# Sparse attention with a feed-forward layer: one register load for the six sampled blocks of a tile

## The chip, the cores and the metric

The kernel runs on one core of one Trainium2 chip. The metric is the device time of that core in microseconds; a result is the median of several runs. A core has engines that run their own instruction streams side by side: PE multiplies matrices, DVE, ACT and POOL do elementwise work, and SP only issues transfers. They wait for one another through semaphores, and each works through its own queue strictly in order.

## The reference

Four batches, eight heads, 768 positions, head width 64. Attention is block sparse in blocks of 32 (24 blocks): a query block sees its own block and its two neighbours, the first and the last block, and three sampled blocks; the first and the last query block see everything. The output goes through a feed-forward layer without residual.

```
scores = scale * np.matmul(q, k.transpose(0, 1, 3, 2))
...
for qb in range(n_blocks):
    for kb in sampled_blocks[qb]:
        mask[qb * block:(qb + 1) * block, kb * block:(kb + 1) * block] = True
scores = np.where(mask, scores, -1000000000.0)
...
attn = attn / (np.sum(attn, axis=-1, keepdims=True) + 1e-09)
return np.matmul(attn, v).astype(np.float32)
...
h = x @ w_in
g = np.maximum(0.01 * h, h)
return (g @ w_out).astype(np.float32)
```

The sampled block numbers are an input of shape 24 x 3, int64, so their values are known only when the kernel runs.

## The kernel before, in words

**Tiles.** Two query blocks (64 queries) make a tile. Each batch has 12 tiles: tile 0 holds the first and the last query block and works on all keys; tiles 1 to 11 work on 12 gathered key blocks each, called slots: four of the window (0 to 3), the first and the last block (4, 5) and six sampled ones, three for each query block (6 to 11). So there are 4 x 11 = 44 gathered tiles. A tile is worked on in four units, one for each pair of heads; four tiles make an item, and an item's feed-forward work is done in chunks while later tiles are in attention.

**A unit's path.** Scores on PE (line 628), scale and mask with the row minimum on DVE (637), exponential on ACT (648), the sums' reciprocal on DVE (657), the high half of the normalised probabilities on ACT (663) and their low half on DVE (668), a transposing transfer issued by SP (671), and the product with V on PE (689). Numbers are kept as a high and a low half-precision part. The feed-forward layer has its matmuls in lines 724 and 751, with work on ACT, DVE and POOL between them (731, 735, 740, 741).

**The K gather** (`gather_k`, lines 558 to 582) fills one of two SBUF buffers: DVE copies the window (564), and POOL copies the six sampled blocks (573), each from a position in the transposed keys that stands in a register. For each slot, POOL first loads the register from the table `offs` (572) and checks its range. The function is a generator that yields after every slot; two slots are taken at each step of the main loop.

**The V gather** (`gather_v`, lines 587 to 605) fills one of two SBUF buffers from a scratch copy of V in HBM. SP issues one transfer for the window (593), at each buffer's first use in a batch two for the first and the last block (598), and then, slot by slot, a register load with its check (601) and the transfer that uses it (603).

**The table.** `build_masks` (199) shifts the block numbers left by five on DVE into `offs` (200), 72 words in the order of the input.

**What sets the order.** The builder is given the work in the order in which the main loop writes it, with priorities by step, and fixes each engine's queue before the run. `in_order` (540) adds an order without a semaphore: all instructions of a new group except the last come after the last instruction of the group before the previous one. A group here is one slot: its load, its check and its copy or transfer. A load can so be at most two slots ahead of its use. SP's queue also carries every other transfer: the loads of q, k, v and the weights (455, 464, 405, 286), the transposes of q and k (517, 494) and of the probabilities (671), the swapped copy of q (519, 520), the store of V's scratch (435) and of the results (775 to 779).

Of the kernel before, what the change touches and what calls it, by code (L numbers as in the profile page):

```python
# [14 lines left out]
I32 = mybir.dt.int32  # L15
AF = mybir.ActivationFunctionType
ALU = mybir.AluOpType
# [3 lines left out]
BLOCK = 32  # L21
# [5 lines left out]
SLOTS = 12  # L27
# [34 lines left out]
def tile_block_sparse_attention_ffn(  # L62
# [19 lines left out]
    nc = tc.nc  # L82
    B, H, S, D = q.shape
    DM, FF = w_in.shape
    NB = S // BLOCK
    NR = sampled.shape[1]
# [5 lines left out]
    NT = NB // 2  # L92
# [7 lines left out]
    cst = ctx.enter_context(tc.tile_pool(name="cst", bufs=1))  # L100
# [12 lines left out]
    def bank(name, tag="h"):  # L113
        return ps_1.tile([P, 512], F32, tag=tag, name=name, bufs={"h": 3, "av": 1}[tag])
# [70 lines left out]
    row = tmps[:1, 6:6 + 2 * NB * NR].bitcast(I32)  # L185
    eq = tmps[:NB, 150:150 + NR * NB].rearrange("p (r b) -> p r b", r=NR)
    sels = [tmps[:NB, 222 + P * a:222 + P * (a + 1)].rearrange("p (a b c) -> p a b c", a=2, b=2) for a in range(2)]
    assert 222 + 2 * P <= DM and 6 + 2 * NB * NR <= 150
    offs = cst.tile([1, NB * NR], I32, name="offs")
    mask = cst.tile([P, NT - 1, SLOTS], F32, name="mask")  # L190

    def load_constants():
# [4 lines left out]
        nc.sync.dma_start(out=sb, in_=sampled.bitcast(I32))  # L197

    def build_masks():
        nc.vector.tensor_scalar(  # L200
            out=offs, in0=row.rearrange("p (a b) -> p a b", b=2)[:, :, 0], scalar1=5, scalar2=None,
            op0=ALU.logical_shift_left)
        sf = cst.tile([NB, NR], F32, name="sf")
        nc.vector.tensor_copy(out=sf, in_=sb.rearrange("p (a b) -> p a b", b=2)[:, :, 0])

        ok = cst.tile([NB, NR], F32, name="ok")
        hit = cst.tile([NB, NB], F32, name="hit")
        for r in range(NR):
            nc.vector.tensor_scalar(out=eq[:, r, :], in0=iota, scalar1=sf[:, r:r + 1], scalar2=None, op0=ALU.is_equal)
            nc.vector.tensor_tensor(out=hit, in0=eq[:, r, :], in1=allow, op=ALU.mult)  # L210
            nc.vector.tensor_reduce(out=ok[:, r:r + 1], in_=hit, op=ALU.add, axis=AX.X)
            nc.vector.tensor_tensor(out=allow, in0=allow, in1=eq[:, r, :], op=ALU.max)
        nc.vector.tensor_scalar(out=ok, in0=ok, scalar1=-1.0, scalar2=1.0, op0=ALU.mult, op1=ALU.add)

        at = cst.tile([NB, NT - 1, 2, NR], F32, name="at")
        nc.gpsimd.affine_select(
            out=at.rearrange("p t a r -> p (t a) r"), in_=ok.unsqueeze(1).to_broadcast([NB, NB - 2, NR]),
            pattern=[[-1, NB - 2], [0, NR]], base=-1, channel_multiplier=1,
            compare_op=ALU.is_equal, fill=0.0)
        pm = bank("mask_ps")[:, :(NT - 1) * 2 * NR].rearrange("p (t a r) -> p t a r", t=NT - 1, a=2)  # L220
        for a in range(2):
            sel = sels[a]
            nc.vector.memset(sel, 0.0)
            nc.vector.memset(sel[:, :, a, :], 1.0)
            nc.tensor.matmul(
                pm[:, :, a, :], sel.rearrange("p a b c -> p (a b c)"), at[:, :, a, :], start=True, stop=True)
        nc.vector.tensor_scalar(
            out=mask[:, :, 6:], in0=pm.rearrange("p t a r -> p t (a r)"), scalar1=-1.0, scalar2=-NEG,
            op0=ALU.add, op1=ALU.mult)
        nc.vector.memset(mask[:, :, :6], 0.0)  # L230
        for hh in range(2):
            a, b = (slice(D * hh + BLOCK * i, D * hh + BLOCK * (i + 1)) for i in range(2))
            nc.vector.memset(mask[a, :, 3:4], NEG)
            nc.vector.memset(mask[b, :, 0:1], NEG)
            nc.vector.memset(mask[a, 0:1, 4:5], NEG)
            nc.vector.memset(mask[b, NT - 2:NT - 1, 5:6], NEG)
# [300 lines left out]
    kgs, vgs = {}, {}  # L537
    last_use = {}

    def in_order(key, begin):  # L540

        new = nc.cur_bb.bb.instructions[begin:]
        last = last_use.setdefault(key, deque())
        if len(last) > 1:
            for i in new[:-1]:
                tc.add_manual_dep(i, last[0], mybir.DependencyInfo(
                    mybir.DependencyClass.NoSync, mybir.DependencyReason.DATA), reason="order")
            last.popleft()
        last.append(new[-1].name)

    def sampled_of(T):

        return [(6 + a * NR + r, (2 * T - 1 + a) * NR + r) for a in range(2) for r in range(NR)]

    kgb = [pa.tile([P, H, KEYS], F16, tag=f"kg{i}", name=f"kg{i}", bufs=1) for i in range(2)]
    ends = {}
# [1 line left out]
    def gather_k(b, T):  # L558

        kt = kts[b]  # L560
        n = (b * (NT - 1) + T - 1) % 2
        kg = kgb[n]
        t0 = (T - 1) * Q2
        nc.vector.tensor_copy(out=kg[:, :, :P], in_=kt[:, :, t0:t0 + P])
        if ends.get(n) != b:
            ends[n] = b
            nc.vector.tensor_copy(
                out=kg[:, :, P:P + Q2].rearrange("p h (n l) -> p h n l", l=BLOCK),
                in_=kt.rearrange("p h (n l) -> p h n l", l=BLOCK)[:, :, 0:NB:NB - 1, :])
        for slot, i in sampled_of(T):  # L570
            begin = len(nc.cur_bb.bb.instructions)
            off = nc.gpsimd.value_load(offs[:1, i:i + 1], min_val=0, max_val=S - BLOCK)
            nc.gpsimd.tensor_copy(  # L573
                out=kg[:, :, slot * BLOCK:(slot + 1) * BLOCK], in_=kt[:, :, bass.ds(off, BLOCK)])
            in_order("k", begin)
            yield
        em = pa.tile([P, KEYS], BF16, tag="em", name=f"em_{b}_{T}", bufs=2)
        nc.gpsimd.tensor_copy(
            out=em.rearrange("p (n l) -> p n l", l=BLOCK),
            in_=mask[:, T - 1, :].unsqueeze(2).to_broadcast([P, SLOTS, BLOCK]))  # L580
        kgs[b, T] = kg, em
        yield
# [4 lines left out]
    def gather_v(b, T):  # L587

        n = (b * (NT - 1) + T - 1) % 2
        vg = vgb[n]  # L590
        t0 = (T - 1) * Q2
        place = lambda slot: (slice(slot % 4 * BLOCK, (slot % 4 + 1) * BLOCK), slot // 4)
        nc.sync.dma_start(out=vg[:, 0, :], in_=scr[b][t0:t0 + P, :])
        if vends.get(n) != b:
            vends[n] = b
            for slot, a in ((4, 0), (5, S - BLOCK)):
                ps, c = place(slot)
                nc.sync.dma_start(out=vg[ps, c, :], in_=scr[b][a:a + BLOCK, :])
        for slot, i in sampled_of(T):
            begin = len(nc.cur_bb.bb.instructions)  # L600
            off = nc.sync.value_load(offs[:1, i:i + 1], min_val=0, max_val=S - BLOCK)  # L601
            ps, c = place(slot)
            nc.sync.dma_start(out=vg[ps, c, :], in_=scr[b][bass.ds(off, BLOCK), :])  # L603
            in_order("v", begin)
        vgs[b, T] = vg.rearrange("p c (h x) -> p c h x", h=H)


# [306 lines left out]
    def start_gather(b, T):  # L914
        for hp in range(NP):
            until(("k", b, hp), lambda: (b, hp) in kready)
        gens["kg", b, T] = gather_k(b, T)
        gathers.append(gens["kg", b, T])
# [4 lines left out]
    def start_gather_v():  # L923
        b, T = vq.popleft()
        until(("v", b), lambda: (b, "ready") in scr)
        assert vfree[0] > 0
        vfree[0] -= 1
        gather_v(b, T)
# [14 lines left out]
    for hp in range(NP):  # L943
        load_v(0, hp)
    build_masks()
    start_k(0, 2)
    start_k(0, 3)
# [49 lines left out]
    for u in units:  # L997
        it, ui = u.item, u.k * NP + u.hp
        b, nb = it.b, it.b + 1
# [7 lines left out]
        if nb < B:  # L1007
            g = it.j * 16 + ui
            t = g - (CFG["k_at"] if b else CFG["k_at0"])
# [4 lines left out]
            t = g - CFG["v_at"]  # L1014
# [135 lines left out]
```

## Time and profile before

| what | value |
|---|---|
| runs of the kernel before | 957.5 us median (956.35, 957.5, 960.08) |
| the profiled execution, span from the first to the last instruction | 959.4 us |
| the profiled execution's own time as shown beside it | its span, 959.4 us; nothing further is listed |
| mean granted TensorE clock in it | 0.934 |
| register loads of lines 601 (SP) and 572 (POOL) | 264 each |
| transfers of line 603 (SP), copies of line 573 (POOL) | 264 each |
| transposes of line 671 (SP) | 208 |

The profile lists, for one execution, the busy time of each engine, the chain of work that ended last (followed back from the last instruction to whatever released it), the costliest groups of instructions, who waited for whom, and the transfers. PE is the matmul part of TensorE and PEld its weight loads, which overlap. Instructions that move registers, branch, signal or issue transfers are not counted as busy, so SP's and POOL's queues of such instructions (SPq, POOLq) are seen only in the chain, in the rows of one line and in the timeline. Idle time of an engine that is not the bottleneck costs nothing. L601 is line 601 of the kernel.

### The profile page before, as it was taken

The numbers are of one execution on the slowest core, as the hardware profiler recorded it, in microseconds if no ns is written. First come the engines' busy times: TensorE is split into PE (matmuls) and PEld (weight loads), VectorE is DVE, ScalarE is ACT, GpSimd is POOL, SyncE is SP. The second block draws the span as 40 slices with busy tenths as digits, with TensorE's granted clock in tenths as the row PEclk, the third lists the DMA queues.
The fourth block names the chain that finished last, engine by engine and source line by source line (L and its number), as shares of the span: only waits on it lengthen the run. The fifth ranks groups of instructions, "written<-read, shape, count | busy, mean of one in ns | idle before, by whom it ended". The sixth has DMA issues, their size and how long they took to land.

```text
span 959.4 us, 21885 instructions
## 1 busy us (share of the span) xinstructions
PE 775.6 (81%) x7020; PEld 485.8 (51%) x7020; DVE 609.4 (64%) x1643; ACT 493.8 (51%) x1061; POOL 328.3 (34%) x469
## 2 busy tenths in 40 slices
PE   1325445878988989997988979897989999999998
PEld 1213233535556555554655545555555655655675
DVE  4986778897576957455766556556666566655221
ACT  4564774755564646445545545555555554545121
POOL 0133544562213424423422344332423334432221
PEclk9996555999998999998999999998998999999999
DMA  9995986957767676685676868766785755556200
GB/s 212 279 269 117 271 169 141 204 113 151 152 167 147 125 147 148 147 146 122 134 175 133 161 121 144 164 135 132 162 164 104 151 135 131 119 114 124 34 23 23
DMA packets 336625, 139.39 MB, mean 145 GB/s; under 512 B 299389, under 2 KB 311678, under 8 KB 336510
## 3 DMA queue, kind: packets, MB, share of 16 engines
q1 hardware_dynamic: 336510, 137.99, 67.8%
q8 instruction: 55, 0.90, 0.4%
q14 instruction: 60, 0.49, 0.2%
HBM read 65.57 MB, written 12.58 MB: 81 GB/s over the span
## 4 chain that ended last, share of the span: by engine, by line
PE 41%; DMA 19%; DVE 16%; SPq 9%; issue 7%; ACT 7%; POOL 0%; ACTq 0%; DVEq 0%
PE h L724 17%; PE o L751 15%; DMA pt<-pp 9%; PE s L628 4%; PE av L689 4%; DVE pp L668 3%; DMA kt<-k_k 3%; DVE p L637 3%; SPq L601 2%; ACT p L648 2%; DMA qs_q<-qa_q 2%; ACT pp L663 2%; SPq L603 2%; SPq L671 2%; DMA W<-in_moe_w_in_dram 1%
## 5 line engine op out<-in xcount | busy, mean ns | idle before, releaser
L724 PE MATMUL h<-x,W 128*128 128x256 f16 x2304 | 288.0, 280 | 1.7 <-DVE k_tot L136 1.2
L751 PE MATMUL o<-W,g 128*128 128x512 f16 x1152 | 280.0, 384 | 4.8 <-DVE g L740 2.7
L724 PEld LDWEIGHTS <-W 128*128 128x128 f16 x2304 | 225.1, 101 | 52.9 <-issue 11.0
L668 DVE SCALAR_TENSOR_TENSOR pp<-p,r,pp 128x384 f16<-128x384 f32 x208 | 151.6, 737 | 128.2 <-ACT pp L663 127.5
L741 POOL TENSOR_TENSOR g<-ht,g 128x512 f16<-128x512 f32 x96 | 115.1, 1199 | 263.6 <-DVE g L740 170.7
L663 ACT ACTIVATE pp<-p,r 128x384 f16<-128x384 f32 x208 | 122.0, 608 | 143.2 <-DMA pt<-pp 111.9
L648 ACT ACTIVATE p<-p,mx 128x384 f32<-128x384 f32 x208 | 126.4, 608 | 98.2 <-DVE mx L637 61.6
L573 POOL COPY kg<-kt 128x256 f16 x264 | 128.5, 508 | 133.9 <-PE s L628 73.2
L751 PEld LDWEIGHTS <-g 128*128 128x128 f16 x1152 | 103.3, 98 | 135.0 <-issue 22.8
L689 PE MATMUL av<-pt,vg 128*64 128x128 f16 x2112 | 100.7, 231 | 47.6 <-DMA pt<-pp 44.8
L637 DVE CUSTOM_DVE_ANT_0 p<-s,em,nsc 128x384 f32<-128x384 f32 x176 | 106.1, 609 | 33.2 <-PE s L628 32.5
L689 PEld LDWEIGHTS <-vg 128*64 128x64 f16 x2112 | 79.5, 115 | 88.8 <-issue 76.4
L735 DVE SCALAR_TENSOR_TENSOR ht<-h,gd,ht 128x512 f32<-128x512 f32 x80 | 59.6, 746 | 54.8 <-ACT ht L731 54.7
L709 POOL TENSOR_TENSOR x<-xf,x 128x256 f16<-128x256 f32 x48 | 34.4, 717 | 155.8 <-ACT x L707 155.8
L731 ACT ACTIVATE ht<-h,gs 128x512 f32<-128x512 f32 x80 | 54.0, 675 | 56.2 <-PE h L724 45.2
L628 PE MATMUL s<-kg,qs_q 128*64 128x384 f16 x352 | 66.4, 368 | 17.9 <-DVE mx L637 15.1
L628 PEld LDWEIGHTS <-qs_q 128*64 128x64 f16 x416 | 27.8, 114 | 92.5 <-issue 70.4
L628 PE MATMUL s<-kg,qxs_q 128*64 128x384 f16 x352 | 63.7, 350 | 6.9 <-DMA qxs_q<-qs_q 6.9
L740 DVE CAST g<-ht 128x512 f16<-128x512 f32 x96 | 41.7, 435 | 8.9 <-PE o L751 7.8
L628 PE MATMUL s<-kt,qs_q 128*64 128x384 f16 x64 | 12.8, 396 | 35.0 <-DVE mx L637 19.7
L648 ACT ACTIVATION_READ_ACCUMULATOR p<-p,mx 128x1 f32 x208 | 39.0, 187 | 0.0
L356 POOL TENSOR_TENSOR W<-W 128x1024 f16<-128x1024 f32 x12 | 28.8, 2409 | 28.5 <-ACT W L355 22.0
(126 smaller groups left out, 727.1 us busy)
## 6 DMA issues: line engine op xcount, KB each, us to landing
vg<-scr SPq DMA_DIRECT2D x280, 64.0 KB, 1.9
vg<-scr SPq DMA_DIRECT2D x44, 256.0 KB, 3.1
v<-in_v_dram SPq DMA_DIRECT2D x32, 192.0 KB, 4.0
qxs_q<-qs_q SPq DMA_DIRECT2D x48, 128.0 KB, 2.4
scr<-v SPq DMA_DIRECT2D x16, 384.0 KB, 3.5
W<-in_moe_w_in_dram SPq DMA_DIRECT2D x5, 1024.0 KB, 7.2
rq<-in_q_dram SPq DMA_DIRECT2D x20, 256.0 KB, 3.9
out_dram<-ob SPq DMA_DIRECT2D x20, 256.0 KB, 2.8
```

Source lines behind the costliest of these rows:

```text
L573: nc.gpsimd.tensor_copy(out=kg[:, :, slot * BLOCK:(slot + 1) * BLOCK], in_=kt[:, :, bass.ds(off, BLOCK)])
L628: nc.tensor.matmul(sp[hh * D:(hh + 1) * D, :], st[:, h, c0:c0 + Q2], keys, start=(n == 0), stop=(n == 1))
L637: nc.vector.tensor_tensor_reduce(out=u.p[i], in0=u.sp[i], in1=kgs[u.b, u.T][1] if u.T else zero.to_broadcast([P, KEYS]), scale=u.nsc, scal ...
L648: nc.scalar.activation(u.p[i], u.p[i], AF.Exp, scale=-1.0, bias=u.mx[:, :1], accum_out=u.pair.sum[:, u.pi, i:i + 1])
L663: nc.scalar.activation(pp[:, 0, :], p, AF.Copy, scale=u.r)
L668: nc.vector.scalar_tensor_tensor(out=pp[:, 1, :], in0=p, scalar=u.r, in1=pp[:, 0, :], op0=ALU.mult, op1=ALU.subtract)
L689: nc.tensor.matmul(pr.av[hh * D:(hh + 1) * D, u.hp], vt[:, l * D:(l + 1) * D], u.pt[c // NCH][:, :, c % NCH, hh * D:(hh + 1) * D], start=( ...
L724: nc.tensor.matmul(c.ph[:, i], W16[:, 2 * b, d, wl, o:o + P], it.x[:, xl, d, :], start=(d == 0 and m == 0), stop=(d == NP - 1 and m == 2))
L731: nc.scalar.activation(c.t, c.ph, AF.Copy, scale=scale[1])
L735: nc.vector.scalar_tensor_tensor(out=c.t, in0=c.ph, scalar=scale[0], in1=c.t, op0=ALU.mult, op1=ALU.max)
L741: nc.gpsimd.tensor_tensor(out=c.g[:, 1], in0=c.t, in1=c.g[:, 0], op=ALU.subtract)
L751: nc.tensor.matmul(it.po[t], c.g[:, gl, i, t * P:(t + 1) * P], W16[:, 2 * (f // PER) + 1, f % PER, wl, :], start=(c.first and i == 0 and m ...
```

## The change

The table gets one row of eight words for each gathered tile, of which six are used. DVE clears it, clamps the block numbers of tiles 1 to 11 to the range 0 to 23 and shifts them. Each gather then loads its tile's six numbers with one call into six registers, on POOL for K and on SP for V, with no check of each value. The group that `in_order` orders is now a whole tile's gather: the load and the first five copies or transfers come after the last one of the tile two before.

```diff
-    offs = cst.tile([1, NB * NR], I32, name="offs")
+    offs = cst.tile([1, NT - 1, 8], I32, name="offs")
...
     def build_masks():
+        blocks = row.rearrange("p (a b) -> p a b", b=2)[:, NR:NR + (NT - 1) * 2 * NR, 0]
+        nc.vector.memset(offs, 0)
         nc.vector.tensor_scalar(
-            out=offs, in0=row.rearrange("p (a b) -> p a b", b=2)[:, :, 0], scalar1=5, scalar2=None,
-            op0=ALU.logical_shift_left)
+            out=offs[:, :, :2 * NR], in0=blocks.rearrange("p (t a) -> p t a", a=2 * NR), scalar1=0, scalar2=NB - 1,
+            op0=ALU.max, op1=ALU.min)
+        nc.vector.tensor_scalar(out=offs, in0=offs, scalar1=5, scalar2=None, op0=ALU.logical_shift_left)
...
-    def in_order(key, begin):
+    def in_order(key, new):
-
-        new = nc.cur_bb.bb.instructions[begin:]
         last = last_use.setdefault(key, deque())
...
-    def sampled_of(T):
+    def sampled_of(T, engine):
-        return [(6 + a * NR + r, (2 * T - 1 + a) * NR + r) for a in range(2) for r in range(NR)]
+        _, rows = nc.values_load_multi_w_load_instructions(
+            offs[:1, T - 1, :2 * NR], engines={engine}, min_val=0, max_val=S - BLOCK,
+            skip_runtime_bounds_check_because="the block numbers are clamped to the sequence before they are shifted")
+        return list(zip(range(6, SLOTS), rows))
...
-        for slot, i in sampled_of(T):
-            begin = len(nc.cur_bb.bb.instructions)
-            off = nc.gpsimd.value_load(offs[:1, i:i + 1], min_val=0, max_val=S - BLOCK)
+        begin = len(nc.cur_bb.bb.instructions)
+        new = []
+        for slot, off in sampled_of(T, mybir.EngineType.Pool):
             nc.gpsimd.tensor_copy(
                 out=kg[:, :, slot * BLOCK:(slot + 1) * BLOCK], in_=kt[:, :, bass.ds(off, BLOCK)])
-            in_order("k", begin)
+            new += nc.cur_bb.bb.instructions[begin:]
             yield
+            begin = len(nc.cur_bb.bb.instructions)
+        in_order("k", new)
...
-        for slot, i in sampled_of(T):
-            begin = len(nc.cur_bb.bb.instructions)
-            off = nc.sync.value_load(offs[:1, i:i + 1], min_val=0, max_val=S - BLOCK)
+        begin = len(nc.cur_bb.bb.instructions)
+        for slot, off in sampled_of(T, mybir.EngineType.SP):
             ps, c = place(slot)
             nc.sync.dma_start(out=vg[ps, c, :], in_=scr[b][bass.ds(off, BLOCK), :])
-            in_order("v", begin)
+        in_order("v", nc.cur_bb.bb.instructions[begin:])
```

## The prediction

> **What bounds the kernel now.** I read the page first (busy time by engine, then the chain of work that ended last), then busy time by stretch, then SP's own timeline, then the rows of the lines that the change touches, and last the table of who waited for whom.
>
> ```profile
> PE 775.6 (81%) x7020; PEld 485.8 (51%) x7020; DVE 609.4 (64%) x1643; ACT 493.8 (51%) x1061; POOL 328.3 (34%) x469
> PE 41%; DMA 19%; DVE 16%; SPq 9%; issue 7%; ACT 7%; POOL 0%; ACTq 0%; DVEq 0%
> PE h L724 17%; PE o L751 15%; DMA pt<-pp 9%; PE s L628 4%; PE av L689 4%; DVE pp L668 3%; DMA kt<-k_k 3%; DVE p L637 3%; SPq L601 2%; ACT p L648 2%; DMA qs_q<-qa_q 2%; ACT pp L663 2%; SPq L603 2%; SPq L671 2%; DMA W<-in_moe_w_in_dram 1%
> 80.00:200.00 120.00, 65.47 (x643) 43.72 (x644) 93.95 (x220) 77.31 (x152) 57.84 (x68) 0.66 0.79 177
> 200.00:890.00 690.00, 620.51 (x5721) 382.99 (x5719) 439.88 (x1223) 361.38 (x817) 242.00 (x366) 0.97 0.68 141
> ```
>
> The first row is busy time and share; the second and third are the chain by engine and by line; the last two give, for a stretch, its length and the busy time of PE, PEld, DVE, ACT and POOL, then granted clock, DMA share and GB/s. From 200 to 890 us PE is busy 620.5 of 690 us, so only 69.5 us are idle; from 80 to 200 it is 54.5 of 120. PE alone holds 41% of the chain, so it is nearly the bound, and the rest of the chain is landings (DMA), DVE and SP's queue. SP does not appear in the busy table, because issuing and register instructions are not counted there. Its timeline has to be read by itself:
>
> ```profile
> 410.52 0.58 SPq L520 DMA_DIRECT2D qxs_q<-qs_q  x1
> 411.20 0.54 SPq L593 DMA_DIRECT2D vg<-scr  x1
> 412.80 5.86 SPq L603 DMA_DIRECT2D vg<-scr  x6
> 418.70 1.01 SPq L405 DMA_DIRECT2D v<-in_v_dram  x2
> 419.82 1.27 SPq L671 DMA_TRANSPOSE pt<-pp  x1
> 421.19 1.45 SPq L494 DMA_TRANSPOSE kt<-k_k  x1
> 422.74 1.54 SPq L671 DMA_TRANSPOSE pt<-pp  x1
> 424.34 1.36 SPq L405 DMA_DIRECT2D v<-in_v_dram  x2
> ...
> 429.16 0.53 SPq L593 DMA_DIRECT2D vg<-scr  x1
> 430.56 6.29 SPq L603 DMA_DIRECT2D vg<-scr  x6
> ```
>
> Columns are start and duration. Each issue begins about 0.1 us after the one before it ended: SP never rests here. The gap of 1.06 us between 411.74 and 412.80 is the first slot's register work, which this merged view leaves out. One V gather (L603 with its register loads) holds SP from 411.74 to 418.70, 6.96 us, and the next gather starts 17.96 us after this one. So well over a third of SP's time goes to gathers, and everything else that SP issues, the probability transposes L671 above all, stands behind them. What that lateness costs is in the table of waits (total us, times, longest):
>
> ```profile
> PE av L689 <- DMA pt<-pp: 62.0, 35, 7.1
> ACT pp L663 <- DMA pt<-pp: 111.9, 64, 4.5
> PE s L628 <- DMA qs_q<-qa_q: 11.6, 4, 9.6
> PE s L628 <- DMA qxs_q<-qs_q: 8.1, 6, 2.3
> PEld L689 <- DMA pt<-pp: 7.1, 3, 5.4
> ```
>
> PE waits 62.0 + 11.6 + 8.1 + 7.1 = 88.8 us in all for transfers that SP issues. Nobody on PE waits for the gathered V itself; the gather hurts through what is queued behind it.
>
> **The change part by part.**
>
> ```profile
> L601 SPq TENSOR_LOAD <-offs x264: 263/273/871, 27.3 to 887.9; - x132
> L601 SPq FUSED_REGOPS  x264: 152/152/184, 27.8 to 888.3; - x132
> L601 SPq SEQ_ASSERT  x264: 18/18/28, 28.1 to 888.5; - x132
> L603 SPq FUSED_REGOPS  x264: 37/37/52, 72.7 to 888.5; - x132
> L603 SPq MOVE vg<-scr x264: 29/29/38, 72.8 to 888.6; - x132
> L603 SPq DMA_DIRECT2D vg<-scr x264: 315/316/993, 72.9 to 888.7; - x132
> L671 SPq DMA_TRANSPOSE pt<-pp x208: 1209/1251/2777, 62.9 to 891.8; - x104
> 343.85 0.27 SPq L601
> 344.11 0.05 issue
> 344.16 0.15 SPq L601
> 344.31 0.05 issue
> 344.36 0.02 SPq L601
> 344.38 0.05 issue
> 344.43 0.04 SPq L603
> ```
>
> The first seven rows give count, then min/median/max ns and first and last start. The last seven are the chain inside one gather: between any two SP instructions lie some 0.05 us.
>
> *SP, removed.* Of six loads a tile, all six checks go (FUSED_REGOPS 152 and SEQ_ASSERT 18), and six TENSOR_LOADs become one. Six old slots cost 6 x (0.273 + 0.152 + 0.018) = 2.66 us and 18 gaps of 0.05 us, 0.90 us: 3.56 us a tile. As a check on the method: adding 6 x (0.037 + 0.029 + 0.316) = 2.29 us and 18 more gaps, 0.90, gives 6.75 us, against the 6.96 us read off the timeline.
>
> *SP, added.* One load of six words, which this trace does not show. It cannot be free; its low end is the row of one word, 0.27 us, its high end is six of those, 1.64 us. I take 0.27, because the nearest row is one TENSOR_LOAD instruction, and the six words lie side by side in one partition. With its gap, 0.32 us (high end 1.69). Net: 3.56 - 0.32 = 3.24 us a tile, at the other end 1.87; over 44 tiles 143 us (82 us) of SP's time. The Trainium skill, in "Runtime: NRT & Kernel Launch", section "Instruction fetch mechanics", says that a register load costs about 200 ns a register even in bulk, which speaks against this half of the change: as an estimate from that figure six words take 1.2 us and the SP saving is about 102 us. No row here has more than one word, so the trace cannot decide it.
>
> *How much of that reaches the end.* Two readings. The chain has 2% of 959.4 us in L601, 19.2 us, which is 19.2 / 0.443 = 43 old loads of the 264, with 3 gaps each: 25.7 us. Their replacement is 43 / 6 = 7.2 new loads, 2.3 us. So the chain by itself promises 23 us (13.5 us at the high price of the load). That counts only gathers that ended last. Since SP has no rest between gathers, time saved at any gather stays saved for all that queues behind, so the second reading goes by what PE waits for: 88.8 us over transfers that SP issues. The 35 waits for transposes average 1.8 us, and a gather returns 3.24 us, so a wait with a gather just ahead of it disappears; one that follows a run of transposes (1.251 us each) does not. I take half: 44 us. What is late next is then DVE and ACT, at 64% and 51%, and PE itself. I forecast the middle of 23 and 44, which is 33 us.
>
> *Behind a wait.* The old loads waited for nothing but the shifted table, and the new one likewise; the gather's first DMA waits for the V buffer as before, with the same transposes behind it. The order rule changes from "the load of a slot after the DMA two slots back" to "the load and the first five DMAs after the last DMA two tiles back", which is no tighter than the queue itself.
>
> *POOL.* The same edit with nearly the same prices:
>
> ```profile
> L572 POOLq TENSOR_LOAD <-offs x264: 281/289/1014, 15.9 to 851.7; - x132
> L573 POOL COPY kg<-kt x264: 388/401/1456, 43.7 to 853.1; 128x256 f16 x132
> L741 POOL TENSOR_TENSOR g<-ht,g 128x512 f16<-128x512 f32 x96 | 115.1, 1199 | 263.6 <-DVE g L740 170.7
> L200 DVE TENSOR_SCALAR offs<-tmps x1: 186/186/186, 15.7 to 15.7; 1x72 int32<-1x72 int32 x1
> ```
>
> Some 3 us a tile come off POOL's sequencer. I cost it at nothing: POOL is busy 34% and holds 0% of the chain, and its other large group, the low half of g, idles 170.7 us waiting for DVE. That cover gone, with POOL the last to arrive, the prize would be up to 44 x 3 us, but nothing on the chain points there.
>
> *DVE.* A memset and one more tensor_scalar of one partition, once: at 0.186 us for the row of the old one, under 0.4 us, hidden because POOL's first load is at 15.9 us but its first copy comes only at 43.7 us. Uncovered it would cost 0.4 us.
>
> **Sum.** The profiled execution spans 959.4 us, within the three runs (956.35 to 960.08); I take the 33 us from the median, 957.5: 924.5, say 925 us.
>
> **The rivals.**
> *A, the load stays dear or is built as several.* If six words cost six loads, or stay six instructions, only checks and gaps go: 1.87 us a tile, 13.5 us by the chain, 20 to 25 us by the second reading in the same proportion. About 938 us. For it: a TENSOR_LOAD brings one word in every row. Against: the instruction named in the diff takes a row of six.
>
> *B, hidden anyway.* PE is the bound, at 620.5 of 690 us, and in the stretches where FFN matmuls follow each other the transposes' lateness is covered. Then only a few us come through: 955 us. For it: 41% of the chain on PE. Against it: 62.0 us of PE waiting for transposes. The Trainium skill says in "DMA: Bandwidth & Descriptors", section "Issuing engines are not separate DMA queues", that the sequencer time for starting a DMA is usually small beside the DMA itself; by that rule this rival would be right. The trace disagrees for these transposes:
>
> ```profile
> pt<-pp SPq DMA_TRANSPOSE x208, 2.9
> ```
>
> 1.251 us of issue stand beside 2.9 us from issue to landing.
>
> *C, slower: the gather is placed too early.* The builder fixes each queue's order ahead of time. If, with cheaper loads, it puts a tile's gather a step earlier, the first DMA stands at SP's head waiting for PE to finish with the buffer, and the transposes wait behind it. A tile has four such steps, 17.96 / 4 = 4.5 us each. The change is lost from a wait of 3.24 us a tile on; at 4.5 us a tile each gather costs 1.3 us more than today. The chain holds 43 of 264 slots, 7.2 gathers' worth, so by it that is 9 us: 967 us; were every gather to count, as they do for a queue without rest, 57 us. For it: SP's order is strict, and the saving is of the same size as a step. Against it: SP is now so late that its gathers hardly ever wait for PE, and a gather one step earlier would mostly find the buffer free.
>
> **How the numbers follow.** Half a per cent, 4.8 us, is about what a measurement of this kernel can tell from no change. Forecast 0.70, A 0.10, B 0.12, C 0.08. The forecast's own spread runs from the 13.5 us of the dear load to 69.5 us, all of PE's idle time from 200 to 890 us: 944 to 888. The range goes up to 952 to take in A and the lower part of B. It leaves out C, the rest of B and a little below 888. Faster by over 0.5% has the forecast, A and a quarter of B: 0.83. Same has the rest of B: 0.09. Slower has C: 0.08.
>
> **What would show it.** Right: the load line has 44 rows of TENSOR_LOAD on SP instead of 264, no FUSED_REGOPS or SEQ_ASSERT there; six gather DMAs take near 3.5 us instead of 6.9; SP's time shows rests between issues; PE av <- DMA pt falls to about half of 62.0 us and ACT pp <- DMA pt from 111.9 us too; PE's idle time from 200 us on shrinks. The step from SP time to end time is wrong if those waits fall and PE's idle time does not, because another releaser (DVE mx, DVE g) takes them. The load's price is wrong if its median is above 0.5 us. Rival C shows as SP waits in front of L593 or L603 of several us. The whole is wrong if the time is over 952 us.

## The result, and the profile after

| kernel | median, us | lowest to highest | profiled span |
|---|---|---|---|
| before | 958.14 (4 runs) | 956.35 to 960.08 | 959.4 |
| changed | 917.85 (4 runs) | 916.94 to 925.11 | 916.0 |

The ratio is 0.9592, with a 95% interval of 0.9552 to 0.9633: 40 us off. The prediction was 925 us with a range of 888 to 952.

First the new load line and the transfer line of the changed kernel (count, min/median/max ns, first and last start):

```profile
L555 POOLq TENSOR_LOAD <-offs x44: 773/780/1506, 22.8 to 807.3; - x44
L555 SPq TENSOR_LOAD <-offs x44: 719/732/1411, 72.1 to 839.5; - x44
L609 SPq FUSED_REGOPS  x264: 37/37/51, 73.1 to 843.0; - x132
L609 SPq MOVE vg<-scr x264: 29/29/42, 73.2 to 843.1; - x132
L609 SPq DMA_DIRECT2D vg<-scr x264: 315/316/1693, 73.3 to 843.2; - x132
```

The loads went from 264 to 44 on each queue, the checks are gone, and the three rows of the transfers stand as before. Six words cost 0.732 us on SP, where one cost 0.273, so the five further words add some 0.09 us each.

SP's timeline in the changed kernel (start, duration) shows what came of it:

```profile
404.77 1.32 SPq L785 DMA_DIRECT2D out_dram<-ob  x2
406.19 0.41 SPq L600 DMA_DIRECT2D vg<-scr  x1
406.65 1.37 SPq L677 DMA_TRANSPOSE pt<-pp  x1
409.73 3.48 SPq L609 DMA_DIRECT2D vg<-scr  x6
413.33 3.90 SPq L677 DMA_TRANSPOSE pt<-pp  x3
417.29 2.33 SPq L467 DMA_DIRECT2D rk<-in_k_dram  x4
419.73 1.81 SPq L677 DMA_TRANSPOSE pt<-pp  x1
423.91 1.23 SPq L520 DMA_TRANSPOSE qs_q<-qa_q  x1
```

Six gather transfers take 3.48 us instead of 5.86. From 421.54 to 423.91 SP issues nothing for 2.4 us: it has caught up and waits for its next operand, which it never did in the stretch shown of before.

The whole trace says the same, from 20 us to the end of the last transpose. Call SP occupied while an instruction of its queue runs and in the gaps under 0.15 us between them. Call it at rest in longer gaps and in semaphore instructions that last over 0.06 us, which are waits. Before, SP was occupied for 854 us and at rest for 20; now it is occupied for 728 us and at rest for 99.

The page's busy row and the chain by engine, then the busy time by stretch (columns as in the prediction), then the table of waits (us in total, times, longest):

```profile
PE 763.0 (83%) x7020; PEld 487.5 (53%) x7020; DVE 618.3 (67%) x1645; ACT 492.9 (54%) x1061; POOL 319.6 (35%) x469
PE 50%; DVE 17%; DMA 14%; issue 8%; ACT 6%; SPq 5%; POOL 0%; POOLq 0%; ACTq 0%; DVEq 0%
```

```profile
200.00:850.00 650.00, 604.57 (x5709) 382.80 (x5706) 433.64 (x1189) 357.26 (x812) 235.55 (x366) 0.97 0.73 148
```

```profile
ACT pp L669 <- DMA pt<-pp: 41.2, 27, 4.5
PE av L695 <- DMA pt<-pp: 23.7, 17, 9.7
PE s L634 <- DVE mx L643: 45.9, 21, 8.8
PE s L634 <- DMA qs_q<-qa_q: 11.1, 2, 8.6
PE s L634 <- DMA qxs_q<-qs_q: 1.2, 1, 1.2
PEld L695 <- DMA pt<-pp: 0.4, 1, 0.4
```

The waits of PE that the prediction added up to 88.8 us are 23.7 + 11.1 + 1.2 + 0.4 = 36.4 us now. ACT's wait for transposes fell from 111.9 to 41.2 us. SP's queue went from 9% of the chain to 5%, transfers from 19% to 14%, and PE from 41% to 50%. The last transpose of the probabilities starts earlier by the whole gain, and the feed-forward work behind it has about kept its length:

```profile
L677 SPq DMA_TRANSPOSE pt<-pp x208: 1210/1234/4892, 62.1 to 846.3; - x104
```

It was 891.8 us before, so 45.5 us earlier; from there to the end are 69.7 us, against 67.6.

### The profile page after: what moved, and what is told of

Read it like the earlier page. It is cut to its first block, busy times and chain, and to the rows that moved or that the text cites. A ratio compares the mean times of both kernels' runs of the same rounds, so it can differ in the third digit from the quotient of the medians.

```text
span 916.0 us, 20401 instructions
## 1 busy us (share of the span) xinstructions
PE 763.0 (83%) x7020; PEld 487.5 (53%) x7020; DVE 618.3 (67%) x1645; ACT 492.9 (54%) x1061; POOL 319.6 (35%) x469
## 4 chain that ended last, share of the span: by engine, by line
PE 50%; DVE 17%; DMA 14%; issue 8%; ACT 6%; SPq 5%; POOL 0%; POOLq 0%; ACTq 0%; DVEq 0%
PE h L730 20%; PE o L757 19%; DMA pt<-pp 6%; PE s L634 5%; PE av L695 4%; DVE p L643 3%; DMA qs_q<-qa_q 3%; DVE pp L674 3%; DMA kt<-k_k 2%; ACT pp L669 2%; DVE W L299 2%; DVE ht L741 1%; SPq L609 1%; ACT p L654 1%; DVE W L296 1%
## 5 line engine op out<-in xcount | busy, mean ns | idle before, releaser
L730 PEld LDWEIGHTS <-W 128*128 128x128 f16 x2304 | 225.8, 100 | 55.8 <-issue 11.1
L578 POOL COPY kg<-kt 128x256 f16 x264 | 114.5, 479 | 122.4 <-PE s L634 100.5
L669 ACT ACTIVATE pp<-p,r 128x384 f16<-128x384 f32 x208 | 118.5, 606 | 69.4 <-DMA pt<-pp 41.2
L695 PE MATMUL av<-pt,vg 128*64 128x128 f16 x2112 | 96.4, 230 | 11.9 <-DVE xf L707 6.9
L695 PEld LDWEIGHTS <-vg 128*64 128x64 f16 x2112 | 77.5, 115 | 51.3 <-issue 42.0
L662 DVE TENSOR_SCALAR sum<-sum 128x2 f32<-128x2 f32 x96 | 26.2, 273 | 15.1 <-ACT p L654 14.5
```

What stands on the lines that cost most here:

```text
L578: nc.gpsimd.tensor_copy(out=kg[:, :, slot * BLOCK:(slot + 1) * BLOCK], in_=kt[:, :, bass.ds(off, BLOCK)])
L669: nc.scalar.activation(pp[:, 0, :], p, AF.Copy, scale=u.r)
L695: nc.tensor.matmul(pr.av[hh * D:(hh + 1) * D, u.hp], vt[:, l * D:(l + 1) * D], u.pt[c // NCH][:, :, c % NCH, hh * D:(hh + 1) * D], start=( ...
L730: nc.tensor.matmul(c.ph[:, i], W16[:, 2 * b, d, wl, o:o + P], it.x[:, xl, d, :], start=(d == 0 and m == 0), stop=(d == NP - 1 and m == 2))
```

## The experiments

Four theories stood against one another. *Theory 1:* SP's queue time at the V gather is what was paid for, and the time follows it in proportion. *Theory 2:* POOL's side brings the gain. *Theory 3:* the builder, which plans every queue ahead, made a better order. *Theory 4*, added after the first four runs: time follows SP's work us for us while SP has no rest, and then another limit of the built order decides. Theory 3 has to be taken seriously: of SP's 789 transfers only 470 stand in the old sequence.

**One side alone.** `k_only` keeps V as before, `v_only` keeps K as before. Each undoes one half of the edit; shown for K, which is the edit of `v_only`:

```diff
-        for slot, off in sampled_of(T, mybir.EngineType.Pool):
+        for i, slot in enumerate(range(6, SLOTS)):
+            begin = len(nc.cur_bb.bb.instructions)
+            off = nc.gpsimd.value_load(offs[:1, T - 1, i:i + 1], min_val=0, max_val=S - BLOCK)
...
+            in_order("k", nc.cur_bb.bb.instructions[begin:])
```

> The changed kernel with the V gather as before (six checked loads on SP per tile); only POOL's loads stay merged and unchecked. Theory 1 (SP's queue time at the V gather): nothing gained, 955 to 962 us, and SP without rest from 80 to 890 us as before. Theory 2 (POOL's side brings the gain): near 918 to 935 us. Theory 3 (the builder's new order of the queues brings it): SP's built order here has 766 of its 789 transfers in the same sequence as before, so 955 to 962 us too; this run parts theory 2 from the others only.

Measured: 960.29 us, ratio 1.001 (0.9986 to 1.0033). SP's timeline of it and its wait:

```profile
423.82 0.53 SPq L600 DMA_DIRECT2D vg<-scr  x1
425.24 6.29 SPq L610 DMA_DIRECT2D vg<-scr  x6
```

```profile
PE av L696 <- DMA pt<-pp: 62.1, 34, 6.3
```

The gather is back at 6.29 us and PE's wait at 62.1: POOL's side alone brings nothing. Theory 2 is out.

> The changed kernel with the K gather as before (six checked loads on POOL per tile); SP's loads stay merged and unchecked. Theory 1: the whole gain, 914 to 924 us. Theory 2 (POOL): 940 us or more. Theory 3 (order): SP's built order shares 663 of 789 transfers in sequence with the changed kernel's, so about 918 us, with no claim on a few us.

Measured: 915.05 us, 0.9543 (0.9521 to 0.9565). The whole gain is SP's side; POOL's loads add nothing that can be measured.

**Half of the change on SP.** `v_checked` loads six words at once for V but checks each value; K's loads stay unchecked:

```diff
+    def checked_of(T, engine):
...
+        _, rows = nc.values_load_multi_w_load_instructions(
+            offs[:1, T - 1, :2 * NR], engines={engine}, min_val=0, max_val=S - BLOCK)
+        return list(zip(range(6, SLOTS), rows))
...
-        for slot, off in sampled_of(T, mybir.EngineType.SP):
+        for slot, off in checked_of(T, mybir.EngineType.SP):
```

> The changed kernel, but the six values of the V gather are still checked on SP after the one load. Six checks of 0.152 + 0.018 us and two gaps of 0.05 us each put 1.62 us a tile back on SP, 71 us over 44 tiles, of the 122 us that the change took off (3.56 less the measured load of 0.73 and its gap, times 44). Theory 1, in proportion to SP time (40 us of time for 122 us of SP): 941 us, 935 to 948. Theory 3 (order): SP's built order shares 664 of 789 transfers in sequence with the changed kernel's, so about 918 us.

Measured: 921.24 us, 0.9624 (0.9591 to 0.9657). The value checks stand in its rows, and the load is dearer too:

```profile
L562 SPq FUSED_REGOPS  x264: 147/147/184, 27.5 to 829.2; - x132
L562 SPq SEQ_ASSERT  x264: 18/18/28, 27.7 to 829.4; - x132
L562 SPq TENSOR_LOAD <-offs x44: 717/1122/2507, 26.5 to 820.8; - x44
```

So some 2 us a tile of register work went back onto SP (1.122 + 6 x 0.265 + 0.05 = 2.76 us a tile against 0.78), 87 us over 44 tiles by these medians. By the whole trace SP is occupied for 798 us, 70 more than in the changed kernel, and at rest for only 29. The time rose by 3 us, which the two intervals do not tell from nothing. Proportion fails here: what the change takes off SP beyond this point turns into rest. Theory 3 had said about 918 us as well, so this run does not part it from theory 4; the next runs on the order do.

`v_six` is the other half: six loads of one word without checks.

```diff
-        for slot, off in sampled_of(T, mybir.EngineType.SP):
+        for i, slot in enumerate(range(6, SLOTS)):
+            begin = len(nc.cur_bb.bb.instructions)
+            _, (off,) = nc.values_load_multi_w_load_instructions(
+                offs[:1, T - 1, i:i + 1], engines={mybir.EngineType.SP}, min_val=0, max_val=S - BLOCK,
+                skip_runtime_bounds_check_because="the block numbers are clamped to the sequence before they are shifted")
...
+            in_order("v", nc.cur_bb.bb.instructions[begin:])
```

> The changed kernel, but the V gather loads its six numbers one by one, each without a check: the checks' removal alone. SP's register work per tile is 6 x (0.273 + 0.05) = 1.94 us, against 3.56 before and 0.78 with the one load; 71 us less than before over 44 tiles. Theory 1, in proportion (40 us for 122 us): 935 us. Theory 4 (each us off SP's queue is a us of time while SP never rests, until another limit of the built order takes over, near 918 us for the changed kernel's order and 894 for the old one): 958 - 71 = 887, so the other limit decides, 890 to 921 us, and the checks alone already bring what the whole change brings.

Measured: 920.26 us, 0.9618 (0.9593 to 0.9642). Either half alone brings nearly the whole gain, within the 890 to 921 us of theory 4.

**The old order.** Two loads that nothing uses stand ahead of each V transfer while the order is made, and are dropped from the program afterwards:

```diff
         for slot, off in sampled_of(T, mybir.EngineType.SP):
+            for _ in range(2):
+                _, (x,) = nc.values_load_multi_w_load_instructions(
+                    offs[:1, T - 1, slot - 6:slot - 5], engines={mybir.EngineType.SP}, min_val=0, max_val=S - BLOCK,
+                    skip_runtime_bounds_check_because="the value is not used")
```

> The changed kernel's instructions in nearly the old order: while the order is made, two more loads stand ahead of each V transfer, which are dropped afterwards since nothing uses them. The built program has the changed kernel's 44 loads and 264 register operations on SP, but its SP transfers share 721 of 789 in sequence with the kernel before (the changed kernel: 470). Theory 1 (SP time): 918 us, 912 to 928. Theory 3 (the new order brings the gain): 950 to 960 us.

Measured: 894.49 us, 0.9321 (0.929 to 0.9352), which neither theory had forecast. The trace, of the slowest of the four runs (902.87 us), corrects the premise: the dropped loads leave a semaphore instruction each.

```profile
L609 SPq EVENT_SEMAPHORE  x528: 17/17/17, 28.0 to 826.5; - x176
```

With gaps of 0.05 us that is 35 us of SP's queue in excess of the changed kernel's, and the kernel is nevertheless 23 us faster. So theory 3 is not only out but the wrong way round: against this order the new one costs. Near the old order, taking 122 - 35 = 87 us off SP brought 64 us.

**A third order.** The same edit with one load in place of two:

> The changed kernel's instructions in a third order: while the order is made, one more load stands ahead of each V transfer, dropped afterwards. Same 44 loads and 264 register operations on SP; SP's transfers share 476 of 789 in sequence with the kernel before and 491 with the changed kernel. It shows how far orders scatter when SP's work is the same: theory 4 has SP's bound at 958 - 122 = 836 us, so every order is at its own limit, between 885 and 930 us. If the old order is special, about 918 us; if the changed kernel's order is a poor draw, about 895 us.

Measured: 906.61 us, 0.9475 (0.945 to 0.9501). It lies between the two forecasts. It carries 264 such leftovers, 18 us of queue. Three orders with short register work give 894, 907 and 918 us.

**SP's time put back.** The extra loads with their value checks, which stay in the program:

```diff
         for slot, off in sampled_of(T, mybir.EngineType.SP):
+            nc.sync.value_load(offs[:1, T - 1, slot - 6:slot - 5], min_val=0, max_val=S - BLOCK)
```

> The changed kernel with SP's time put back: ahead of each V transfer stands one more load of one word with its check, whose value nothing uses. SP's register work per tile is 0.78 + 3.56 = 4.34 us, 0.78 us more than before the change, 34 us over 44 tiles. SP's built order has 694 of 789 transfers in the sequence of the kernel before. Theory 1, in proportion (0.33 us for each us of SP): 969 us. Theory 4 (us for us while SP has no rest): 985 to 995 us, with SP without rest. Theory 3 (order alone): about 958 us.

Measured: 976.75 us, 1.0215 (1.0177 to 1.0252), beside 956.71 us for the kernel before. Its waits:

```profile
ACT pp L670 <- DMA pt<-pp: 134.4, 66, 5.6
PE av L696 <- DMA pt<-pp: 67.3, 38, 6.8
```

With nothing added but register work on SP, and an order again close to the old one (694 of 789), the changed kernel becomes slower than before, and the same two waits grow beyond the old 111.9 and 62.0 us. By the rows 34 us of work cost 20 us, between theories 1 and 4. But the rows overstate it: over the whole trace SP is occupied for 873 us, 19 more than before and 27 more than in `k_only`, mostly because issuing its transfers other than transposes took 234 us in all, against 247 and 242. Counted like this the time follows SP's work nearly us for us, with 14 us of rest, as theory 4 has it.

**SP relieved without touching the gather.** In the kernel before, ACT issues the raw loads of K and V:

```diff
-            nc.sync.dma_start(out=t[:, :, h, :], in_=v[b, 2 * hp + h].rearrange("(c p) d -> p c d", p=P))
+            nc.scalar.dma_start(out=t[:, :, h, :], in_=v[b, 2 * hp + h].rearrange("(c p) d -> p c d", p=P))
...
-            nc.sync.dma_start(out=t[:, h], in_=k[b, 2 * hp + h].rearrange("(c p) d -> p c d", p=P))
+            nc.scalar.dma_start(out=t[:, h], in_=k[b, 2 * hp + h].rearrange("(c p) d -> p c d", p=P))
```

> The kernel before with its loads untouched, six checked loads a tile, but the 64 loads of raw K and V are issued by ACT: 37 us of issue and some 6 us of gaps leave SP's queue. It asks whether SP's queue is the limit by itself. Theory 1 as the runs so far size it (about half a us of time for each us of SP's work): 958 - 22 = 936 us, plus up to 5 us for ACT, 930 to 945 us. Theory 4 (us for us): 915 to 920 us. Theory 3 (only the order counts; SP's transfers that stay share 619 of 725 in sequence with the kernel before): 950 to 965 us.

Measured: 945.12 us, 0.9864 (0.9814 to 0.9914). With the register loads and value checks all in place, PE's wait falls, and ACT's does not:

```profile
ACT pp L663 <- DMA pt<-pp: 127.3, 75, 4.8
PE av L689 <- DMA pt<-pp: 25.0, 18, 4.6
```

So SP's queue costs time even with the gather untouched, but less than us for us came through here: SP is occupied for 822 us, 32 less, and the time fell by some 13 us, just short of what theory 1 allowed (930 to 945 us). ACT now issues 64 transfers and may have taken part of the gain; that is not shown.

**The same relief where SP has rest.** The ACT edit on top of the 894 us version:

> The instructions in nearly the old order as in the earlier run of 894 us, and the 64 loads of raw K and V (0.58 us of issue each, 37 us, with gaps 43 us) are issued by ACT instead of SP. SP's transfers that stay share 684 of 725 in sequence with that run. If SP's time still bounds that kernel, 855 to 875 us. If the other limit has taken over, as its 41 us of rest on SP say, 885 to 900 us; ACT loses as much as SP gains, and ACT at 55% has room but its steps stand between DVE's, so up to 10 us slower is possible.

Measured: 899.58 us, 0.9402 (0.9375 to 0.9428), against 894.49 us without the edit: no gain. SP's occupied time fell from 764 to 723 us and its rest grew from 51 to 85 us. Where SP rests, taking more off its queue buys nothing, and the same edit that helped the kernel before helps no more.

**One number of the plan.** The raw V loads come two units later, before and after the change:

```diff
-    "v_at": 28,
+    "v_at": 30,
```

> The kernel before with one number of its plan changed: the raw V of the next batch is loaded two units later (30 instead of 28). The work is the same; SP's transfers share 742 of 789 in sequence with the kernel before. It shows how far the time moves with the order alone while SP has no rest: since SP's work sets the pace, little, 952 to 964 us.

> The changed kernel with the same number changed (30 instead of 28). SP's transfers share 718 of 789 in sequence with the changed kernel. With SP's work out of the way the order should count for more: 900 to 925 us. If the changed kernel's order is no poorer than others, 915 to 921 us.

Measured: 958.37 us before the change, 0.999 (0.9966 to 1.0013), and 912.85 us after it, 0.9496 (0.9451 to 0.9541). While SP's queue sets the pace, this order change moves nothing; once it does not, it may be worth some 5 us.

The runs together, by SP's register work per tile (loads, checks, leftovers and their gaps, from the medians of the rows above), with SP's occupied time and rest in the whole trace as defined above. Each trace is one execution:

| kernel | SP register work a tile, us | SP occupied, us | SP at rest, us | ratio to before |
|---|---|---|---|---|
| put_back | 4.34 | 873 | 14 | 1.0215 |
| before | 3.56 | 854 | 20 | 1 |
| k_only | 3.56 | 846 | 23 | 1.001 |
| v_checked | 2.76 | 798 | 29 | 0.9624 |
| v_six | 1.94 | 785 | 45 | 0.9618 |
| old_order | 1.58 | 764 | 51 | 0.9321 |
| third_order | 1.18 | 739 | 77 | 0.9475 |
| after_v30 | 0.78 | 730 | 92 | 0.9496 |
| v_only | 0.78 | 731 | 96 | 0.9543 |
| changed | 0.78 | 728 | 99 | 0.9592 |

From 4.34 down to 2.76 us the time falls by 6%, and SP's rest stays under 30 us. Below that the rest grows, and the time no longer follows the work but the order, over a spread of 3%.

## Why the prediction was right, step by step

*SP's queue never rests, and the gather hurts through what stands behind it:* right. SP rested for 20 us of 873. `v_only` has the whole gain, `k_only` none, and `put_back` turns it into a loss.

*The load's price:* mis-sized. I took 0.27 us, the row of one word; it is 0.732. The net saving is 3.56 - 0.78 = 2.78 us a tile, 122 us, not 143. The Trainium skill's 200 ns a register, in "Runtime: NRT & Kernel Launch", section "Instruction fetch mechanics", is also off for this load: 0.732 us for six is 0.122 each. (The page gives its figure beside the register loads that the runtime adds; this one reads a table in SBUF.) With the load and its gap the whole gather in the timeline above holds SP for 3.48 + 0.78 = 4.26 us, not for the 3.5 us of the forecast, against 6.96 before. The mis-sized load did not matter for the time, since `v_checked` with a load of 1.122 us and all its checks loses only 3 us.

*How much reaches the end:* the first reading, 23 us by L601's share of the chain, was too low, because the chain follows one path and counts a gather only where it ended last. The second reading, half of 88.8 us of PE's waits, 44 us, was close to the 40 measured, and the middle of the two made the forecast 7 us too slow. That it came so close is in part luck, for the half and the middle were both guesses. The waits themselves fell by more than half, by 52.4 us; part of that came back where the prediction looked for it, at PE s <- DVE mx, 34.8 us before in the same table and 45.9 now:

```profile
PE s L628 <- DVE mx L637: 34.8, 20, 8.2
```

PE's idle time from 200 us on shrank all the same, from 69.5 us (to 890 us) to 45.4 us (to 850 us). These waits are no steady price, though: in `before_act` PE's wait for transposes fell by 37.0 us for some 13 us of time, and in `v_checked` it is 47.9 us, twice that of the changed kernel, for 3 us of time. What the prediction did not size is where SP begins to rest: of some 125 us that left its queue, 79 turned into rest.

*POOL and DVE at nothing:* right for POOL by `k_only`. DVE's three small instructions were not tried alone, but they stand in `k_only` too, which is no slower.

*Rival A, only the checks go:* its price was wrong. `v_six` is that case, and it brings 920 us instead of 938.

*Rival B, hidden anyway:* wrong as a whole, right for the last part: of the time that left SP's queue, the last 70 us, from `v_checked` to the changed kernel, bought only 3. That feed-forward matmuls are what hides them is not shown.

*Rival C, a gather placed too early:* its sign is in the trace. SP's own waits in the changed kernel have a row that was next to nothing before:

```profile
SPq L600 <- PE av L695: 17.3, 7, 4.8
```

SP stands 17.3 us at the gather's first transfer until PE releases the buffer. But the 894 us version has more of it (in the trace of its 902.87 us run),

```profile
SPq L600 <- PE av L699: 28.7, 13, 6.9
```

so the size of that wait does not explain why the new order is the poorer one.

**What stays open.** Which step of the new order costs the 23 us to the near-old one, and so what limits the changed kernel now that SP rests. Most edits of SP's work also changed the order; only `before_v30` and `after_v30` changed the order alone, and by little. The version at 894 us beats both kernels, by an accident of planning.

## What to carry to other kernels

An engine that only issues is not in the busy table: read its timeline, and if its issues follow one another without rest, its register work counts like any other work on the path. Price the gain by the time that leaves that queue, and expect it to stop where the queue begins to rest; here that was after 40 to 64 us of time, depending on the order, and the trace of before does not tell where. The queue's share of the chain gave too little, and the waits for what stands behind it came close in one run and not in others. In a kernel whose queues are planned ahead, a change in an instruction's price also draws a new order, worth up to 3% here: try the new instructions under another order before judging the change.

## What was not expected of the hardware

A load of six words into registers costs 0.732 us on SP and 0.780 us on POOL, against 0.273 and 0.289 for one. The same load had a median of 1.122 us in `v_checked`, where checks surround it. A value check took 0.147 to 0.152 us for its comparison and 0.018 for its assertion, so that six of them with their gaps cost twice as much as the load of all six words. Issuing the same transfers (transposes left out) took SP 234 us in all in `put_back`, 247 before and 257 in the changed kernel; why is not shown.
